# Moving the last batch's first tile forward by one tile, and computing its small second expert on 32 places amid the main one (attention, then a gated mixture of experts, one core)

## The chip, the cores and the metric

The kernel runs on one core of a Trainium2 chip. The metric is device time in microseconds of one execution, lower is better; the median of three runs of the kernel before is 509.26 us (508.65 to 509.94).

## What is computed

Multi-query attention with 8 batches, 16 heads, 384 rows and head size 64 gives 3072 rows of 1024 numbers. Each row then goes to one of 16 experts (4 groups of 4), chosen by two argmaxes; an expert is a two-layer network with a ReLU. Cut to what matters:

```python
attn = softmax(q @ k.T / 8) @ v                 # 8 batches, 16 heads, 384 x 64; one k and v per batch
x = attn.transpose(0, 2, 1, 3).reshape(3072, 1024)
g_idx = argmax(x @ w_group)                     # 4 groups
e_idx = argmax(x @ w_expert[g_idx])             # 4 experts in the group
h = relu(x @ w1[g, e])                          # 1024 x 1024
out = (g_softmax * e_softmax)[:, None] * (h @ w2[g, e])   # 1024 x 1024
```

The inputs are one fixed draw. With it the reference sends all 384 rows of each of batches 0 to 6 to one expert (a different one for most batches), and of batch 7's rows 363 to expert 0 and 21 to expert 2.

## The kernel before

**Tiles and steps.** A tile is 128 rows of one batch, for all 16 heads; there are 24 tiles, t = 0 to 23, three to a batch and in the order of the batches. Each takes four steps of the main loop (L794), so there are 96 steps, i = 0 to 95, with t = i // 4 and p = i % 4. In a step two units are worked on, each two heads of the tile: `scores` (L198, TensorE, L206) puts the scores into one of two PSUM tiles of tag s; `soft` takes the negated row maximum (VectorE, L217) and the exponentials with their sums (ScalarE, L220); `norm` multiplies by the reciprocal sums (GpSimd, L235); and `transp` (VectorE, L241) transposes the units of two steps before into a ring, from which `pv` (TensorE, L257) multiplies them with v, in steps with p of 2 and 3, for the tile before. `pv_out` copies the result out (ScalarE L271, GpSimd L272 into `xb`, the bf16 input of the expert).

**Experts.** In steps with p of 0 and 1 TensorE also works on an expert: `main_expert` is a generator, and `advance(n)` takes 3n portions of it. A batch's expert has 42 portions: three for each of eight 128-wide chunks of the hidden layer (8 matmuls with L479, then a ReLU copy by ScalarE or VectorE, L485/L487), three for each of six pieces of the output (8 matmuls with L493, then a scaled copy into y, L511/L513, and after two pieces the stores, L536). Batch b's expert starts at step 12b + 17, that is 5 steps after the batch's last attention step, so that the 42 portions fit in the steps that follow. The PSUM banks of these matmuls come from a pool of four (`xbank`, tag x) that `pv`, the gate and the expert take in turn; the fifth taker waits until the first one's bank has been read. After the main loop the experts take the s banks instead (`bank_end`).

**Which expert, and when the weights are asked for.** Every batch's main expert is chosen from its first tile alone: `logits` at the batch's step 8, `gate_first`, `gate_choose`, `gate_score` and `gate_pick` at step 9 (L338 to L386), and then `load_main` asks GpSimd's DMA queue for w1 and w2 (L454, two DMAs each, converted to bf16 on the way). The steps are counted from s0 = 12b. The rest of the gate follows when the other two tiles are there (`logits` at s0 + 16, `gate_masks`, `gate_values`, `gate_selected`). For batch 7 a second expert is chosen too (`gate_pick_second`), and its weights are asked for after the main loop (`load_second`, L837 and L844).

**The end, L827 to L908.** After the main loop come the rest of batch 6's expert, the last tile's `pv`, batch 7's gate, batch 7's main expert and, last, the second one. The functions whose names begin with `few_` serve the latter: its rows are gathered into at most 128 places. `few_turn` transposes xb back to rows, `few_flags` and `few_places` give each flagged row its place, `few_gather` (L643) picks the rows with a 0/1 matrix, `few_expert` computes both layers for 128 places (L674, L689) and writes the rows to `out` in DRAM with an indirect DMA by GpSimd (L696). They come after everything else in TensorE's order. Then each engine reads the number of experts left over (L910), and a loop over these (L911) runs as often as that says; in the profiled execution none of its instructions ran.

**What sets the order.** The schedule is by hand: the program's order is each engine's order. `at(step, place, fn, ...)` (L721) puts a function at a step and at one of the places (m0, m1, m3, v, m2, w, e, g) that the loop calls with `run`. "w" stands before `norm`, and "e" and "g" stand behind it.

Of the kernel before, what the change touches and what calls it, by code (L numbers as in the profile page):

```python
# [9 lines left out]
FP32 = mybir.dt.float32  # L10
BF16 = mybir.dt.bfloat16
I32 = mybir.dt.int32
P = 128
# [6 lines left out]
def kernel(  # L20
# [24 lines left out]
    NR = 4096  # L45
    assert NR > N
# [9 lines left out]
    w2f = moe_w2.rearrange("g e (fo fi) d -> (g e) fi fo d", fi=P)  # L56

# [27 lines left out]
    units = [(b, j, c ^ (4 * swapped(b * ST + j))) for b in range(B) for j in range(ST) for c in range(8)]  # L85
# [16 lines left out]
    def load_q(t, first=False):  # L102
        b, j = t // ST, t % ST
# [142 lines left out]
    def pv(t, n0, n1):  # L246

        v_sb = st["v", t // ST]
# [14 lines left out]
    def pv_out(t):  # L263
        b, j = t // ST, t % ST
# [199 lines left out]
    def load_second(n):  # L464
        if n == 0:
            st["e2"] = nc.gpsimd.value_load(st.pop("idx2")[0:1, 0:1], min_val=0, max_val=GE - 1)
        st.setdefault("w_second", []).append(load_w(st["e2"], n))
# [4 lines left out]
    def expert(xb, w1, w2, result, psum, on_act=None):  # L472
# [3 lines left out]
        for fc in range(FO):  # L476
            hp = psum()
            for ko in range(KO):
                nc.tensor.matmul(  # L479
                    out=hp[:, 0:S], lhsT=w1[:, ko, ts(fc, P)], rhs=xb[:, ko, :], start=(ko == 0), stop=(ko == KO - 1)  # L480
                )
                if ko % (KO // 2) == KO // 2 - 1:
                    yield
            if on_act(fc):
                nc.scalar.activation(out=h_t[:, fc, :], in_=hp[:, 0:S], func=ACTF.Relu)  # L485
            else:
                nc.vector.tensor_scalar(out=h_t[:, fc, :], in0=hp[:, 0:S], scalar1=0.0, scalar2=None, op0=ALU.max)  # L487
            yield
# [41 lines left out]

    def main_expert(b, on_act):
        w1, w2 = st.pop(("w", b))

        def store(j, y):
            for n in range(QN):
                nc.sync.dma_start(out=out_v[b, j, n], in_=y[32 * n:32 * (n + 1), :])  # L536

        yield from expert(st["xb", b], w1, w2, scaled(lambda: st["gsel", b][0], store), any_bank, on_act)

    def few_ready():  # L540
# [4 lines left out]
        for name, t, widths in (  # L545
            ("16", c16, (("eye", P), ("tri", P), ("sel", ST * P), ("f", 4), ("cum", 4), ("parts", 5 * ST))),
            ("32", c32, (
                ("cols", P), ("tri", P), ("sel", ST * P), ("prod", ST * GE), ("ohs", GE), ("rows", ST), ("rest", ST), ("row", 1), ("pos", 4),
                ("f", ST), ("fits", 1), ("gate", 1), ("low", 1), ("at", 1),
# [412 lines left out]
```

## Time and profile before

| what | value |
|---|---|
| median of 3 runs | 509.26 us (508.65 to 509.94) |
| the profiled execution's own time | 508.39 us |
| its span (first to last instruction) | 507.0 us |
| granted TensorE clock, mean | 0.997 |
| TensorE, matmuls (PE) | 481.5 us busy, 95% |
| VectorE (DVE) | 413.0 us, 81% |
| ScalarE (ACT) | 321.8 us, 63% |
| GpSimd (POOL) | 289.6 us, 57% |
| bytes moved by DMA | 84.04 MB |

A time in the trace is counted from the span's start. "PE" rows are matmuls, "PEld" rows weight loads, which run beside them. A matmul's row lasts until its last result is written, so the next one starts before it ends: the pace is read from the starts. In the timeline a row merges neighbours: start, length, engine, line, operation, tiles, shapes and count, and in brackets the idle time before it with what ended that. In the chain of work that ended last, each row is a start, a length and what was running.

### The profile page before, as it was taken

To read this page: it belongs to the slowest core of one execution; us is meant where nothing else is said; L and a number is where in the kernel's file an instruction comes from. 1 tells how busy PE (TensorE), PEld (TensorE's weight loads), DVE (VectorE), ACT (ScalarE), POOL (GpSimd) and SP (SyncE) were. 2 spreads that over 40 slices of the span, in tenths; PEclk is the share of its full clock that TensorE was granted. 3 is DMA by queue.
4 is the path that set the end of the run, shared out by engine and by line. 5 is a ranking of instruction groups with operands and counts; after the bars stand their busy time and mean duration, and the time that the engine had idled before them with its cause. 6 is when DMAs were issued, how large, how long until landed. Compare 5 with 4: busy or idle time off the path is not lost.

```text
span 507.0 us, 20054 instructions
## 1 busy us (share of the span) xinstructions
PE 481.5 (95%) x8256; PEld 262.1 (52%) x8273; DVE 413.0 (81%) x737; ACT 321.8 (63%) x1002; POOL 289.6 (57%) x524
## 2 busy tenths in 40 slices
PE   7597789999999999999999999999999999999994
PEld 3143356555456455555465455555455455555653
DVE  3889979988899879988899879998799888890630
ACT  4776766677676766676676776676775775753421
POOL 1665955684576664584576654584476654584300
PEclk9999999999999999999999999999999999999998
DMA  7612997399947998389946998389956993089993
GB/s 106 145 26 45 174 239 193 76 160 233 255 86 129 220 237 218 75 157 232 261 84 123 217 243 223 75 143 230 245 116 111 210 241 110 1 155 241 231 243 121
DMA packets 64524, 84.04 MB, mean 166 GB/s; under 512 B 20379, under 2 KB 39963, under 8 KB 64432
## 3 DMA queue, kind: packets, MB, share of 16 engines
q0 software_dynamic: 19152, 37.84, 41.3%
q1 hardware_dynamic: 44320, 44.61, 35.2%
q8 instruction: 66, 1.08, 0.9%
q10 hardware_dynamic: 960, 0.30, 0.3%
q14 instruction: 26, 0.21, 0.1%
HBM read 101.52 MB, written 19.40 MB: 239 GB/s over the span
## 4 chain that ended last, share of the span: by engine, by line
PE 90%; DVE 5%; ACT 3%; issue 1%; POOL 0%; POOLq 0%; ACTq 0%; DVEq 0%
PE x L257 26%; PE s L206 25%; PE x L479 15%; PE x L493 13%; PE sb L493 4%; PE x L280 3%; ACT pr L220 3%; DVE nmx L217 2%; PE sb L479 2%; DVE ring L241 2%; PE x L674 1%; PE x L100 1%; PE x L689 1%; PE x L145 0%; PE x L643 0%
## 5 line engine op out<-in xcount | busy, mean ns | idle before, releaser
L235 POOL TENSOR_SCALAR pr<-pr,rinv 128x384 f32<-128x384 f32 x384 | 218.3, 588 | 146.0 <-DVE rinv L231 133.2
L220 ACT ACTIVATE pr<-s,nmx 128x384 f32<-128x384 f32 x384 | 218.0, 579 | 131.5 <-DVE nmx L217 120.0
L217 DVE TENSOR_REDUCE nmx<-s 128x2 f32<-128x768 f32 x192 | 174.3, 948 | 45.7 <-PE s L206 44.6
L241 DVE STREAM_TRANSPOSE ring<-pr 128x768 f32<-128x768 f32 x192 | 175.4, 952 | 0.1
L206 PE MATMUL s<-kt,qt 64*64 64x384 f32 x1536 | 148.9, 496 | 13.3 <-ACT pr L220 12.3
L257 PE MATMUL x<-ring,v_sb 32*64 32x256 f32 x4608 | 137.7, 378 | 0.2
L257 PEld LDWEIGHTS x<-ring,v_sb 32*64 32x64 f32 x4608 | 101.6, 131 | 43.0 <-issue 23.2
L206 PEld LDWEIGHTS s<-kt,qt 64*64 64x64 f32 x1536 | 48.5, 132 | 82.6 <-ACT pr L220 44.4
L220 ACT ACTIVATION_READ_ACCUMULATOR pr<-s,nmx 128x1 f32 x384 | 77.9, 203 | 0.0
L479 PE MATMUL x<-xb,w 128*128 128x384 bf16 x448 | 76.6, 326 | 0.0
L479 PEld LDWEIGHTS <-w 128*128 128x128 bf16 x512 | 47.7, 98 | 42.2 <-issue 12.6
L493 PE MATMUL x<-w,h_t 128*128 128x512 bf16 x276 | 64.7, 380 | 0.6
L493 PEld LDWEIGHTS <-h_t 128*128 128x128 bf16 x384 | 35.7, 98 | 52.0 <-issue 11.9
L454 POOL DMA_DIRECT2D w<-in_moe_w_dram x36 | 27.9, 784 | 10.8 <-issue 9.0
L271 ACT COPY xt<-x 128x256 f32<-128x256 f32 x96 | 28.9, 385 | 2.8 <-PE x L257 2.7
L485 ACT ACTIVATE h_t<-x 128x384 bf16<-128x384 f32 x56 | 25.4, 502 | 6.4 <-PE x L479 6.4
L272 POOL CAST xb<-xt 128x1024 bf16<-128x1024 f32 x24 | 24.9, 1036 | 3.6 <-ACT xt L271 3.6
L511 ACT ACTIVATE y<-x,gsel 128x512 f32<-128x512 f32 x36 | 24.8, 693 | 3.1 <-PE x L493 3.1
L195 DVE STREAM_TRANSPOSE qt<-q_sb 128x512 f32<-128x512 f32 x38 | 26.1, 687 | 0.0
L493 PE MATMUL sb<-w,h_t 128*128 128x512 bf16 x92 | 21.2, 379 | 0.2
L231 DVE RECIPROCAL rinv<-ssum 128x4 f32<-128x4 f32 x96 | 13.9, 144 | 3.3 <-ACT pr L220 3.3
L511 ACT ACTIVATE y<-sb,gsel 128x512 f32<-128x512 f32 x9 | 6.2, 688 | 16.1 <-PE sb L493 16.1
(132 smaller groups left out, 165.6 us busy)
## 6 DMA issues: line engine op xcount, KB each, us to landing
w<-in_moe_w_dram POOLq DMA_DIRECT2D x36, 1024.0 KB, 19.6
q_sb<-in_q_dram SPq DMA_DIRECT2D x76, 224.0 KB, 6.0
out_dram<-y SPq DMA_DIRECT2D x96, 128.0 KB, 6.3
xb_scratch<-xb SPq DMA_DIRECT2D x8, 768.0 KB, 4.3
v_sb<-in_v_dram SPq DMA_DIRECT2D x32, 96.0 KB, 4.0
kk<-in_k_dram SPq DMA_DIRECT2D x28, 92.0 KB, 4.1
q_sb<-in_q_dram SPq DMA_DIRECT2D x16, 128.0 KB, 3.3
q_sb<-in_q_dram SPq DMA_DIRECT2D x5, 64.0 KB, 3.1
```

What stands on the lines that cost most here:

```text
L195: nc.vector.transpose(out=qt[:].rearrange("p (x d) -> p x d", d=32), in_=q_sb[:, :, 0:32])
L206: nc.tensor.matmul(out=s[m * D:(m + 1) * D, h, 0:S], lhsT=qt[r, ts(2 * cc + m, D)], rhs=kt[r, :], start=True, stop=True, tile_position=(h ...
L217: nc.vector.tensor_reduce(out=nmx[:], in_=s[:, :, 0:S], axis=AX.X, op=ALU.max, negate=True)
L220: nc.scalar.activation(out=pr[:, h, :], in_=s[:, h, 0:S], func=ACTF.Exp, bias=nmx[:, h:h + 1], scale=1.0, accum_out=ssum[:, k, h:h + 1],)
L235: nc.gpsimd.tensor_scalar(out=pr, in0=pr, scalar1=rinv[:, k, h:h + 1], scalar2=1.0, op0=ALU.mult, op1=ALU.mult)
L241: nc.vector.transpose(out=ring[:, (u // 4) % 3, u % 4].rearrange("p h s -> p (h s)"), in_=st.pop(("pr", u))[:].rearrange("p h s -> p (h s)"),)
L257: nc.tensor.matmul(out=o[i][h * D:(h + 1) * D, 0:2 * P].rearrange("d (g c q) -> d g c q", g=2, c=4), lhsT=v_sb[r, n, :], rhs=ring[r, a:z + ...
L271: nc.scalar.copy(out=xt[:, :, ts(i, 32)], in_=o[:, 0:2 * P].rearrange("p (c q) -> p c q", c=KO))
L454: nc.gpsimd.dma_start(out=w[:, o:o + 4, :], in_=(w1f, w2f)[n][ds(e, 1), :, o:o + 4, :].rearrange("o p c f -> (o p) c f"))
L479: nc.tensor.matmul(out=hp[:, 0:S], lhsT=w1[:, ko, ts(fc, P)], rhs=xb[:, ko, :], start=(ko == 0), stop=(ko == KO - 1))
L493: nc.tensor.matmul(out=yp, lhsT=h_t[:, fo, ts(j, P)], rhs=w2[:, fo, ts(nh, 512)], start=(fo == 0), stop=(fo == FO - 1),)
L511: nc.scalar.activation(out=y[:, ts(nh, 512)], in_=yp, func=ACTF.Copy, scale=g)
```

## The change

Four things change together.

1. **The order of the tiles.** The list `tiles` moves batch 7's first tile ahead of batch 6's third: t = 20 is now (7, 0), t = 21 is (6, 2). `first_slot` and `last_slot` (80 and 92 for batch 7, 72 and 84 for batch 6) replace s0 in the schedule. So batch 7's expert is chosen at step 89 and not at 93; its weights are asked for at steps 89 and 90 (before: 93 and 94). `load_k`, `load_v`, `scale_k` and `k_blocks` of batch 7 move with it; batch 6's later gate steps stay at 92 to 95.
2. **Batch 6's expert in two parts.** It still starts at step 89 with 42 portions, but its input's third tile is now written at the end of step 91. The hidden layer is computed for columns 0 to 255 first (16 portions, in steps 89, 92 and 93) and for columns 256 to 383 then (8 portions of one chunk each, in step 93). TensorE's order shows 32 matmuls of 256 columns in step 89, 24 in step 92, and in step 93 eight of 256 and 64 of 128.
3. **The second expert's weights** are asked for at steps 94 and 95. w2 comes in another layout (`w2r`) and goes to the two q buffers.
4. **The second expert on 32 places, amid the main one.** Its 32 rows are the stationary operand in four column tiles of 32, the weights are the moving one (`few_rows`: 32 matmuls of 256 columns a layer). `few_put` makes the transposed 0/1 matrix, `few_spread` copies each result row to its place in the tile with 12 fp32 matmuls, and the gates and the main expert's rows are joined in SBUF (`last_expert`: y = main * gate + y). The indirect DMA is gone. The ReLU copies of batch 7's expert alternate between ScalarE and VectorE; before, all eight were ScalarE's. The last piece of y is stored by two queues, SP's and ACT's. `keep_xb` of batch 7 goes ahead of its expert.

The diff, cut to its core:

```diff
+    FEW = 32
...
+    w2r = moe_w2.rearrange("g e (fi fo) d -> (g e) fi fo d", fi=P)
...
+    tiles = [(b, j) for b in range(B) for j in range(ST)]
+    tiles.insert(-3, tiles.pop(-3))
+    first_slot = [4 * tiles.index((b, 0)) for b in range(B)]
+    last_slot = [4 * tiles.index((b, ST - 1)) for b in range(B)]
+    units = [(*bj, c ^ (4 * swapped(t))) for t, bj in enumerate(tiles) for c in range(8)]
...
+        halves = [qpool.tile([P, KO // 2, Dm], BF16, tag="q", name="wq", bufs=2) for _ in range(2)]
+        for h, half in enumerate(halves):
+            o = h * (KO // 2)
+            nc.gpsimd.dma_start(
+                out=half[:], in_=w2r[ds(st["e2"], 1), :, o:o + KO // 2, :].rearrange("o p c f -> (o p) c f")
+            )
...
+        for lo, hi, steps in parts:
+            for fc in range(FO):
+                hp = psum()[:, 0:hi - lo]
+                for ko in range(KO):
+                    nc.tensor.matmul(
+                        out=hp, lhsT=w1[:, ko, ts(fc, P)], rhs=xb[:, ko, lo:hi], start=(ko == 0), stop=(ko == KO - 1)
+                    )
+                    if ko + 1 in (KO // 2, KO)[:steps[fc] - 1]:
+                        yield
...
+            *([((0, 2 * P, (3, 2, 2, 2, 2, 2, 2, 1)), (2 * P, S, (1,) * FO))] if b == B - 2 else []),
...
+    def last_expert():
+
+        w1, w2 = st.pop(("w", B - 1))
+        ys = st["ys"] = [pool.tile([P, Dm], FP32, tag="y", name="y", bufs=3) for _ in range(ST)]
+        banks = [bank_end] * FO + [lambda: xbank()[:]] * (2 * ST)
+
+        def result(j, nh, yp, by_act):
+            y, g = ys[j][:, ts(nh, 512)], st["gsel", B - 1][0][:, j:j + 1]
+            if j == 0:
+                nc.scalar.activation(out=y, in_=yp, func=ACTF.Copy, scale=g)
+                return
+            nc.vector.scalar_tensor_tensor(out=y, in0=yp, scalar=g, in1=y, op0=ALU.mult, op1=ALU.add)
+            if j == ST - 1:
+                store_rows(B - 1, j, ys[j], ts(nh, 512), (nc.sync, nc.scalar) if nh else (nc.sync,))
+            elif nh:
+                store_rows(B - 1, j, ys[j])
...
+    def few_rows(lhs, w):
+        bank = xbank()
+        for o in range(KO):
+            for c in range(P // FEW):
+                nc.tensor.matmul(
+                    out=bank[ts(c, FEW), 0:256], lhsT=lhs[:, ts(o, FEW)], rhs=w(o)[:, ts(c, 256)],
+                    start=(o == 0), stop=(o == KO - 1), tile_position=(0, c * FEW),
+                )
...
...
+    def few_hidden():
...
+        bank = few_rows(fw["xg"], lambda o: w1[:, o, :])
+        nc.vector.transpose(
+            out=fw["h32"].rearrange("p (o t) -> p o t", t=FEW), in_=bank.rearrange("p (x o) -> p o x", o=FO)
+        )
+        nc.vector.tensor_scalar(out=fw["h16"], in0=fw["h32"], scalar1=0.0, scalar2=None, op0=ALU.max)
+    def few_out():
...
+        bank = few_rows(fw["h16"], lambda o: halves[o // 4][:, o % 4, :])
+        nc.vector.tensor_copy(out=fw["y32"], in_=bank)
...
+    def few_spread(js):
...
+                nc.tensor.matmul(
+                    out=parts[c // 2][:, c % 2, a:a + 256], lhsT=fw["put32"][r, ts(j, P)], rhs=fw["y32"][r, :],
+                    start=True, stop=True, tile_position=(c * FEW, 0),
+                )
...
+        if last:
+            at(s0 + 9, "w", load_main, b, 0)
+            at(s0 + 10, "w", load_main, b, 1)
+            at(s0 + 13, "w", gate_pick_second, b)
+            at(s0 + 14, "g", load_second, 0)
+            at(s0 + 15, "g", load_second, 1)
...
-    pending.append(main_expert(b, lambda k: k < FO or k % 2 == 0))
+    pending.append(last_expert())
...
     gate_count()
-    advance(1)
+    advance(2)
...
-    advance(3)
     few_gather()
     advance(2)
+    few_put()
+    few_hidden()
+    advance(1)
+    few_out()
+    advance(1)
+    few_spread((0, 1))
+    advance(1)
+    few_spread((2,))
+    advance(1)
...
     advance(1000)
-    keep_xb(b)
-    few_expert()
```

More of the change, by code (lines that the diff above doesn't have):

```diff
@@ L263, in pv_out @@
     def pv_out(t):
[L264 removed]
+        b, j = tiles[t]
         if j < 2:
@@ L683, in few_expert @@
-        cols = ((0, 512), (512, 768), (768, Dm))
-        ys = [xbank()[:, 0:z - a] for a, z in cols]
-        y = pool.tile([P, Dm], FP32, tag="y", name="few_y", bufs=3)
-        for part in range(2):
-            for (a, z), yp in zip(cols, ys):
-                for fo in range(4 * part, 4 * part + 4):
-                    nc.tensor.matmul(
-                        out=yp, lhsT=h_t[:, fo, 0:P], rhs=w2[:, fo, a:z], start=(fo == 0), stop=(fo == FO - 1)
-                    )
-                if part and a:
-                    nc.scalar.activation(out=y[:, a:z], in_=yp, func=ACTF.Copy, scale=gate)
-                elif part:
-                    nc.vector.tensor_scalar(out=y[:, a:z], in0=yp, scalar1=gate, scalar2=None, op0=ALU.mult)
```

192 lines of the change are left out of this document (80 added, 112 removed).

## The prediction

> **What bounds the kernel now.** I read the page first: which engine is busy, and who holds the chain of work that ended last. Then I read the chain's end, and step by step the two stretches that the diff touches.
>
> ```profile
> PE 481.5 (95%) x8256; PEld 262.1 (52%) x8273; DVE 413.0 (81%) x737; ACT 321.8 (63%) x1002; POOL 289.6 (57%) x524
> PE 90%; DVE 5%; ACT 3%; issue 1%; POOL 0%; POOLq 0%; ACTq 0%; DVEq 0%
> ```
>
> TensorE holds nine tenths of the chain, so time taken from its queue is gained and time added is lost, unless another engine is waited for. What matters is the pace of its rows and the few places where it waits. The chain's end (start, length, what):
>
> ```profile
> 481.28 1.34 PE x L643 x24
> 486.20 6.91 PE sb L493 x32
> 493.11 3.57 PE x L674 x64
> 496.95 2.35 PE x L689 x14
> 499.81 0.86 ACT L693 ACTIVATE few_y<-x,c 128x256 f32<-128x256 f32 x2 [2.70 <-PE x L689]
> 501.08 1.05 POOL out_dram L696
> out_dram<-few_y,c POOLq DMA_INDIRECT x1, 2.8
> ```
>
> The second expert stands alone at the end: from 493.11 TensorE does nothing else, ScalarE takes the last piece off by 500.67 (499.81 + 0.86), GpSimd starts the indirect write at 501.02, and it lands 2.8 us later, at 503.8. The span ends at 507.0, 3.2 us behind the landing.
>
> The other stretch is step 93, where batch 6's expert will do nine chunks in place of three. There the profile shows this:
>
> ```profile
> 418.43 1.52 PE L206 MATMUL s<-kt,qt 64*64 64x384 f32 x16
> 423.89 1.52 PE L206 MATMUL s<-kt,qt 64*64 64x384 f32 x16
> 437.19 1.52 PE L206 MATMUL s<-kt,qt 64*64 64x384 f32 x16
> 438.64 2.77 PE L479 MATMUL x<-xb,w 128*128 128x384 bf16 x16
> 439.88 0.21 DVE L290 STREAM_TRANSPOSE lg<-x 128x32 f32<-128x32 f32 x1
> 440.87 0.59 ACT L220 ACTIVATE pr<-s,nmx 128x384 f32<-128x384 f32 x1
> 441.43 0.88 ACT L485 ACTIVATE h_t<-x 128x384 bf16<-128x384 f32 x2
> 442.67 1.52 PE L206 MATMUL s<-kt,qt 64*64 64x384 f32 x16
> ```
>
> TensorE starts the chunks at 438.64, but ScalarE takes the first off only at 441.43, behind the step's four exponentials. The three chunks, 1.3 us each up to 442.67, fit into the four banks, so this delay costs nothing today. The first two rows are the scores of steps 89 and 90; step 89 runs like this one, 18.76 us earlier (418.43 against 437.19).
>
> **The tail, part by part, in the clock of before.** Until the sixth chunk of batch 7's expert nothing changes on TensorE; it is done at about 478.7 (481.28 less two chunks of 1.3). These rows price what follows:
>
> ```profile
> 482.45 0.22 PE L654 MATMUL x<-c 128*128 128x5 bf16 x3
> 468.12 1.10 PE L280 MATMUL x<-xt,wge 128*32 128x64 f32 x64
> 444.12 2.85 PE L257 MATMUL x<-ring,v_sb 32*64 32x256 f32 x96
> L680 DVE TENSOR_SCALAR few_h<-x 128x256 bf16<-128x256 f32 x1 | 0.4, 424 | 1.9 <-PE x L674 1.9
> L513 DVE TENSOR_SCALAR y<-sb,gsel 128x512 f32<-128x512 f32 x3 | 2.3, 751 | 6.9 <-DMA out_dram<-y 2.7 <-PE x L894 2.5 <-PE sb L493 1.7
> 477.27 0.21 DVE L416 TENSOR_REDUCE es<-g_ex 128x15 f32<-128x60 f32 x1
> 482.00 0.35 DVE L887 TENSOR_SCALAR sel<-end,pcum,pw 128x128 bf16<-128x128 f32 x1
> 469.29 0.25 DVE L290 STREAM_TRANSPOSE lg<-x 128x64 f32<-128x64 f32 x1 [12.87 <-PE x L280]
> 493.15 0.75 DVE L513 TENSOR_SCALAR y<-sb,gsel 128x512 f32<-128x512 f32 x1 [2.70 <-DMA out_dram<-y]
> ```
>
> - Gather: 24 matmuls of 32 columns. Of 128 columns they pace at 56 ns (1.34 / 24); three of 5 columns in L654 take 0.22, that is under 40 ns each beyond the last one's run-out. I take 1.0 us (0.9 to 1.34): 479.7. Two chunks of 1.3: 482.3. `few_put`, three at 56 ns: 482.5.
> - `few_hidden`: 32 matmuls in four column tiles of 32. The nearest row is L280, also 32 matmuls in four such tiles, 1.03 us from start to the next start (the row has two records for each). So 1.0 (0.9 for streaming alone, four at once, at the chunks' 384 columns in 0.163 us; 3.5 if they run one after another): 483.5. `few_out` is the same.
> - VectorE now has chunks 1, 3, 5 and 7, a ReLU of 384 columns each: 0.58, between the 0.42 of 256 and the 0.75 of 512. Chunk 5's (478.8 to 479.4) stands ahead of the gate chain, which lasts 5.1 us (477.27 to 482.35, L416 to L887) and includes waits for GpSimd. So it ends at 484.5, and chunk 7's ReLU, queued behind it, at 485.1.
> - Output piece 0 (8 matmuls, 1.73: 6.91 / 4) would run 483.5 to 485.2, but its eighth waits for chunk 7: 485.4. `few_out` waits for `few_hidden`'s transpose (0.42 by L290's 0.25 for 64 columns and 0.69 for L195's 512) and ReLU (0.3) behind that on VectorE: 485.9. So two stalls, 0.7 us together. `few_out` ends at 486.9, piece 1 at 488.6.
> - `few_spread`: 12 fp32 matmuls of 256 columns in four row tiles. L257 does 48 in eight tiles in 2.78, a round of eight in 0.46; a round of four takes the same, so 0.93 and then 0.46. Its copies and joins (two on VectorE, four on ScalarE, about 0.75 each as L513) lie beside pieces 2 and 3. Piece 2 ends at 491.3, the second spread at 491.8, piece 3 at 493.5, pieces 4 and 5 at 497.0.
> - The last join: 0.75, 497.8. SP then issues two stores at 0.42, and ACT two beside it: the last at 498.3. It lands 2.5 us later (2.0 is the least of the 96).
>
> ```profile
> L195 DVE STREAM_TRANSPOSE qt<-q_sb 128x512 f32<-128x512 f32 x38 | 26.1, 687 | 0.0
> L536 SPq DMA_DIRECT2D out_dram<-y x96: 314/419/1085, 113.2 to 495.5; - x96
> DMA to landing us min/median/max: 2.0/6.3/13.9
> out_dram<-y SPq DMA_DIRECT2D x3, 128.0 KB, 2.5
> ```
>
> The landing comes at 500.3 to 500.8, against 503.8; what follows it (3.2) stays. **The tail gains 3.3 us** (2.5 to 4.0). By TensorE alone: it is rid of 7.1 (493.11 to about 500.2, a ScalarE copy before 500.67) and 1.4 of gather, and gets 1.0 + 0.2 + 2.0 + 1.4 and 0.7 of stalls, which is 3.2 less; from its last matmul to the landing it stays at about 3.6.
>
> **Step 93.** Eight chunks of 256 columns pace at 0.87, eight of 128 at 0.45 (8 x 56 ns). Together 10.6 us against 10.4, so the split itself costs 0.2. The banks cost more. Step 93 takes four banks with its first 256-wide and three 128-wide chunks (438.64 + 0.87 + 3 x 0.45 = 440.86; the fourth bank is the logits', free at 440.2 by VectorE's L290, so no wait). The fifth chunk needs the first's bank. ScalarE reads it at 441.43, behind the exponentials, for 0.38 (L682's 256 columns below); so TensorE stands until 441.9. Five chunks of 0.45 then end at 444.15, where the scores of step 94 started at 442.67 before. **Step 93 loses 1.5 us**: 1.0 of waiting and 0.5 of chunks. Step 89 has the 0.4 us less of work, but loses it again: its fourth chunk is the fifth taker (`gate_choose` has a bank too) and waits for ScalarE until 423.05, so it ends at 423.9 as before. Range of this term: 0.5 (no wait) to 2.2.
>
> The Trainium skill's page "TensorE: Matmul & The Clock Gate" (Back-to-back issue gap) gives about 81 ns for a sustained matmul of 128 columns with its weight load. By it the 64 of step 93 would take 5.2 us instead of 3.6, and the sum below would be -0.2 instead of -1.8. L674 in the chain above is 64 matmuls of this very shape, with their loads, in 3.57 us; it gives 56 ns, and I go by it.
>
> ```profile
> L682 ACT ACTIVATE few_h<-x 128x256 bf16<-128x256 f32 x1 | 0.4, 384 | 1.1 <-PE x L674 1.1
> 444.41 1.58 POOL L454 DMA_DIRECT2D w<-in_moe_w_dram  x2 [5.13 <-issue]
> 449.83 4.53 POOL L235 TENSOR_SCALAR pr<-pr,rinv 128x384 f32<-128x384 f32 x8
> 451.45 3.91 DVE L241 STREAM_TRANSPOSE ring<-pr 128x768 f32<-128x768 f32 x4
> 456.41 2.85 PE L257 MATMUL x<-ring,v_sb 32*64 32x256 f32 x96
> DMA to landing us min/median/max: 8.2/19.6/26.7
> L437 POOL TENSOR_TENSOR gate<-gate,gs 128x48 f32<-128x48 f32 x1 | 0.3, 287 | 0.1
> GB/s 106 145 26 45 174 239 193 76 160 233 255 86 129 220 237 218 75 157 232 261 84 123 217 243 223 75 143 230 245 116 111 210 241 110 1 155 241 231 243 121
> ```
>
> **What is moved and costs nothing.** GpSimd waits for the choice and issues the loads ahead of its `norm` (5.13 us idle, 1.58 of issuing); this moves from steps 93 and 94 to 89 and 90. `norm` of 89 then ends some 3 us later, but its transposes come two steps (8 us) later, so it stays hidden. The second expert's loads are behind `gate_values` at step 94 (four small operations like L437, and 1.6 of issuing) and delay `norm` of step 95 to about 456.4, the last transpose to 457.4; the last `pv`, at 456.41 before, is now asked for at 457.9. Hidden by half a microsecond; without that cover it costs up to 1. On VectorE step 93 gets `gate_masks` and `gate_pick_second`, twelve operations of about 0.2 us like L416, and is through at about 444.6, half a microsecond before the next maximum is due (the scores start at 444.15); `gate_selected` at step 95 waits for GpSimd's product (done by then), with only a reciprocal and the transposes behind it. Batch 7's k and v come about a tile earlier too: eight loads on SP, a scaling on GpSimd and one transpose on VectorE (0.6 by L195 and L290), in steps 70 to 76, whose tiles have been read by then; VectorE isn't the bound there. On SP `keep_xb` waits for GpSimd's cast ahead of batch 6's last stores, whose pieces are computed after that cast. The weights: the second expert's w1 is asked for by 454 and w2 by 460, and they are needed at 484.0 and 487.4 (482.5 and 485.9, plus the 1.5 of step 93); the slowest landing of L454 is 26.7. Batch 7's own load moves into a stretch that is free now (the 35th slice, 431 to 444, moves 1 GB/s).
>
> **Sum.** 1.5 - 3.3 = -1.8 us. On the profiled execution: 508.39 - 1.8 = 506.6, a span of 505.2. That execution is 0.87 us below the median of the runs shown, so by the median 509.26 - 1.8: **507.5 us**.
>
> **Rivals.** (a) *The split costs only its columns*: TensorE doesn't stand at step 93, because ScalarE is ahead of where I put it. Then -2.8 to -3.1 (the columns' 0.5 or 0.2): 506.3. For it: TensorE hardly waits for ScalarE today. Against: the fifth taker has no other bank, and the exponentials stand ahead in ScalarE's order. (b) *VectorE becomes the end's bound*: chunk 7's ReLU, `few_hidden`'s two operations and four joins follow the gate chain in one queue, and each microsecond that this is late stops TensorE for as long; with `norm` of 95 late as well, 1.3 us of the gain go: -0.5, 508.8, no change. For it: its 81% of the span, and 0.7 us of stalls by my own count. (c) *The column tiles don't run side by side*: the 64 matmuls of `few_hidden` and `few_out` at 0.108 us are 6.9 us instead of 2.0, which gives +3.1, 512.4, slower. At 0.06 us for a matmul the gain is gone (0.031 + 1.8 / 64), and from 0.083 on it is slower by 0.3%. Against it L280: 64 records in 1.03. The Trainium skill's page "TensorE: Matmul & The Clock Gate" (Part 3, on row and column tiling) says that a weight load overlaps with matmuls in flight only where the row groups differ; here all four tiles share one, which speaks for (c). The trace doesn't bear it out: L280's tiles share the row group too, and its records follow each other at 16 ns (1.03 / 64). (d) *It isn't done as it says*: if over 32 rows were flagged, the expert would go to the loop at the end, with 112 more matmuls (21 us) behind a load (19.6 us): +40. The reference's draw has 21 rows. (e) *The second weights land late*: they would have to take longer than the slowest today; 4 us beyond it give -1.8 + 3.3 (26.7 leaves 0.7 for w2), 510.8.
>
> **How the numbers follow.** Chances: the forecast 0.50, (a) 0.15, (b) 0.22, (c) 0.08, (d) 0.01, (e) 0.04. The forecast's own range is 506.4 to 508.5 (the two terms' ends, rarely both). A measurement of this kernel can tell about 0.3%, 1.5 us, from no change. Two thirds of the forecast and (a) are faster by more: 0.34 + 0.15 = 0.49. The rest of it and (b) are within: 0.38. (c), (d), (e): 0.13 slower. The range leaves out these and the far ends: 505.8 to 510.0.
>
> **What would show it.** Right: in step 93 a gap of about 1 us on TensorE in the middle of the 128-column chunks, ended by ScalarE's ReLU; the column-tiled matmuls of each layer in about 1 us; the last output piece some 3 us earlier against the expert's start than the old `few_expert`'s end; the last store landing about 2.5 us behind its issue. Wrong: no gap at 93 (then a); TensorE waiting for VectorE's transposes or joins by more than 1 us in all (b); pieces of 0.1 us (c); a matmul of the second layer released by a DMA (e).

## The result

The changed kernel takes **512.26 us** (median of 19 runs, 509.67 to 516.03), the kernel before 509.26 (19 runs, 507.51 to 510.62). The ratio is 1.006, with a 95% interval of 1.0042 to 1.0079: it is slower by about 3 us, where 1.8 us less was forecast. Its profiled execution took 513.75 us (span 512.3, granted clock 0.996), against 508.39 (span 507.0, clock 0.997).

The page of the changed kernel, its engines and one group (busy time, mean ns, idle time before it and what ended most of it):

```profile
PE 479.7 (94%) x8320; PEld 262.9 (51%) x8337; DVE 415.9 (81%) x741; ACT 320.8 (63%) x1005; POOL 286.3 (56%) x511
L261 PE MATMUL x<-ring,v_sb 32*64 32x256 f32 x4608 | 137.9, 378 | 3.0 <-issue 2.6
```

TensorE is busy no longer than before (481.5) and yet ends later, so time went into standing still. The rows of what it waited for that bear on this, first of the kernel before, then of the changed one (waiter, releaser: us in total, times, longest). The longest row of both, the scores' waits for ScalarE, is left out; it is 12.3 before and 12.2 now:

```profile
PE s L206 <- issue: 0.8, 1, 0.8
PE x L183 <- issue: 0.7, 1, 0.7
```

```profile
PE x L261 <- issue: 2.6, 3, 1.6
PE x L492 <- ACT h_t L498: 1.2, 2, 0.8
PE x L261 <- DVE ring L245: 0.4, 1, 0.4
```

The wait for ScalarE's ReLU is the forecast one. The waits called "issue" are not: nothing that the profile shows as a semaphore ends them, and all three stand in runs of `pv` matmuls; they follow below. (Two older ones, like the two rows of the kernel before, end at 66 to 75 us in all profiles but those of e7 and d4.) First step 93 of the changed kernel:

```profile
438.85 1.52 PE L210 MATMUL s<-kt,qt 64*64 64x384 f32 x16
440.31 2.39 PE L492 MATMUL x<-xb,w 128*128 128x256 bf16 x32
443.53 2.39 PE L492 MATMUL x<-xb,w 128*128 128x128 bf16 x40 [0.84 <-ACT h_t L498]
445.86 1.52 PE L210 MATMUL s<-kt,qt 64*64 64x384 f32 x16
```

The step lasts 7.00 us (438.85 to 445.86) where it lasted 5.48: 1.52 more, 0.84 of it standing in the middle of the 128-column chunks. Then the tail:

```profile
483.76 0.76 PE L663 MATMUL x<-c,xtok 128*128 128x32 bf16 x24
487.22 1.06 PE L684 MATMUL x<-w,xg 128*32 128x256 bf16 x32
490.72 1.06 PE L684 MATMUL x<-wq,xg 128*32 128x256 bf16 x32 [0.29 <-DVE xg L698]
493.54 1.15 PE L716 MATMUL part<-rest,c 32*128 32x256 f32 x16
494.62 1.90 PE L506 MATMUL x<-w,h_t 128*128 128x512 bf16 x7
495.58 1.35 ACT L726 ACTIVATE y<-part,gsel 128x512 f32<-128x512 f32 x2 [1.24 <-DVE y L728]
496.45 1.22 PE L716 MATMUL part<-rest,c 32*128 32x256 f32 x8
497.61 1.90 PE L506 MATMUL x<-w,h_t 128*128 128x512 bf16 x8
503.13 0.75 DVE L570 SCALAR_TENSOR_TENSOR y<-x,gsel,y 128x512 f32<-128x512 f32 x1 [0.91 <-PEq L945]
503.91 2.25 ACTq L546 DMA_DIRECT2D out_dram<-y  x2
```

A part's price is read from its start to the next part's: gather 0.61, each layer of the small expert 0.99 (487.22 to 488.21, 490.72 to 491.71), first spread 1.08, second 1.16. The last join ends at 503.88. ScalarE's two stores follow at once, SP's two do not:

```profile
507.45 0.78 SPq L546 DMA_DIRECT2D out_dram<-y  x2
```

```profile
SPq L546 <- DMA out_dram<-y: 3.1, 1, 3.1
```

SP stood 3.1 us, until ScalarE's first store had landed (507.38), and its own two landed at 509.06 and 509.52. In the trace the kernel's stores signal their landing on eight semaphores in turn, and SP's next store had the one (number 100) of ScalarE's first: that is what it waited for. The span ends at 512.3, 2.8 us behind the last landing.

So the 5.3 us of span come from these stretches. Up to step 68 the changed kernel is 0.3 ahead (its scores start at 317.64, not 317.92). From there to step 95 (450.13 against 446.90) it loses 3.5: 1.52 in step 93, 1.07 in step 79, 0.66 in step 87, 0.2 in 88, 89 and 92 together. From step 95 to batch 7's second turn of logits (473.23 against 468.12) it loses 1.9, with the 1.57 and the ring's 0.36. From there to the end it takes 39.0 us, not 38.8: of the tail's forecast gain of 3.3 us nothing arrives.

### The profile page after: what moved, and what is told of

Same layout as the page of the kernel before. It is cut to its first block, busy times and chain, and to the rows that moved or that the text cites. A ratio compares the mean times of both kernels' runs of the same rounds, so it can differ in the third digit from the quotient of the medians.

```text
span 512.3 us, 20178 instructions
## 1 busy us (share of the span) xinstructions
PE 479.7 (94%) x8320; PEld 262.9 (51%) x8337; DVE 415.9 (81%) x741; ACT 320.8 (63%) x1005; POOL 286.3 (56%) x511
## 5 line engine op out<-in xcount | busy, mean ns | idle before, releaser
L210 PE MATMUL s<-kt,qt 64*64 64x384 f32 x1536 | 148.9, 496 | 13.5 <-ACT pr L224 12.2
L492 PE MATMUL x<-xb,w 128*128 128x384 bf16 (+2 forms) x512 | 77.1, 306 | 1.2 <-ACT h_t L498 1.2
L506 PE MATMUL x<-w,h_t 128*128 128x512 bf16 x322 | 75.8, 380 | 0.9
L492 PEld LDWEIGHTS <-w 128*128 128x128 bf16 x576 | 51.3, 98 | 40.6 <-issue 14.1
L458 POOL DMA_DIRECT2D w<-in_moe_w_dram x34 | 26.3, 784 | 8.4 <-DVE qt L199 6.0
L498 ACT ACTIVATE h_t<-x 128x384 bf16<-128x384 f32 (+2 forms) x64 | 26.3, 463 | 7.0 <-PE x L492 7.0
L336 POOL TENSOR_TENSOR mask_all<-oh 128x48 bf16<-128x48 f32 x8 | 2.2, 271 | 25.0 <-DVE oh L332 25.0
L284 PEld LDWEIGHTS x<-xt,wge 128*32 128x32 f32 x1024 | 12.8, 110 | 5.5 <-ACT y L524 2.5
```

Source lines behind the costliest of these rows:

```text
L210: nc.tensor.matmul(out=s[m * D:(m + 1) * D, h, 0:S], lhsT=qt[r, ts(2 * cc + m, D)], rhs=kt[r, :], start=True, stop=True, tile_position=(h ...
L458: nc.gpsimd.dma_start(out=w[:, o:o + 4, :], in_=(w1f, w2f)[n][ds(e, 1), :, o:o + 4, :].rearrange("o p c f -> (o p) c f"))
L492: nc.tensor.matmul(out=hp, lhsT=w1[:, ko, ts(fc, P)], rhs=xb[:, ko, lo:hi], start=(ko == 0), stop=(ko == KO - 1))
L498: nc.scalar.activation(out=h_t[:, fc, lo:hi], in_=hp, func=ACTF.Relu)
L506: nc.tensor.matmul(out=yp, lhsT=h_t[:, fo, ts(j, P)], rhs=w2[:, fo, ts(nh, 512)], start=(fo == 0), stop=(fo == FO - 1),)
```

## The experiments

Each ran beside the kernel before on one chip; "before" in the table is its median there.

| run | what it is | median us (runs) | before | ratio, 95% interval |
|---|---|---|---|---|
| e4_order_alone | new order, split and earlier weights; old tail | 511.80 (7) | 509.6 | 1.0030 to 1.0069 |
| e5_tail_alone | new tail, natural order | 521.7 (6) | 509.6 | 1.0205 to 1.0267 |
| e1_sp_alone | changed; last stores on SP alone | 513.46 (6) | 509.6 | 1.0061 to 1.0117 |
| e3_relu_dve | changed; two ReLUs of step 93 on VectorE | 514.2 (6) | 509.6 | 1.0076 to 1.0121 |
| e6_k_early | before; batch 7's k 4 steps earlier | 509.96 (12) | 509.0 | 0.9999 to 1.0037 |
| e7_shifted | changed; +128 TensorE instructions at the start | 526.42 (5) | 509.0 | 1.0303 to 1.0354 |
| e10_whole_block | changed; +256 there | 511.42 (12) | 508.9 | 1.0032 to 1.0081 |
| e8_one_store | changed; a half stored by one DMA | 515.37 (6) | 509.0 | 1.0112 to 1.0160 |
| e9_k_late | changed; batch 7's k back at step 74 | 513.33 (6) | 509.0 | 1.0062 to 1.0137 |
| a0_again | the changed kernel again | 511.56 (12) | 508.9 | 1.0035 to 1.0085 |
| c2_mended | e9 and e1 together | 510.26 (12) | 508.9 | 0.9994 to 1.0041 |
| c1_mended_relu | c2 and e3 | 512.71 (7) | 508.9 | 1.0045 to 1.0097 |
| d1_quarter | c2, +64 instructions behind step 93 | 510.69 (12) | 508.7 | 1.0014 to 1.0054 |
| d2_half | c2, +128 there | 512.57 (6) | 508.7 | 1.0064 to 1.0099 |
| d3_weights_late | c2, second weights later | 510.77 (6) | 508.7 | 1.0029 to 1.0065 |
| d4_relu_half | c1, +128 there | 512.21 (6) | 508.7 | 1.0057 to 1.0098 |

My theories after reading the result: the split's wait in step 93 (B in the expectations); stores at the end that wait for each other (S; SP and ScalarE sharing what the stores signal on); and gaps of TensorE that no semaphore ends (a rival in the first runs, then F if moved transfers make instruction fetches late, G if the place of the instructions does, T if the second weights' transfers do).

**Halving the change.** e4 keeps `before`'s tail and takes the new order; e5 keeps the new tail and drops `tiles.insert(-3, tiles.pop(-3))`, the split and the earlier weights.

> The kernel before (509.26) with the new order of the tiles, batch 6's expert in two parts and batch 7's weights asked for at steps 89 and 90, but with the old end (128 places, indirect write, second weights asked for after the main loop). Theory B (the split alone costs 1.5 us, the earlier request buys nothing, since no matmul waited for these weights): 510.8, step 93 at 7.0 us and the end as before. Rival D (the moved transfers make TensorE's instruction supply stall as well): 512 to 513, with gaps of a microsecond and more that no semaphore ends. Rival G (the earlier weights help the end): below 509.3.

> The changed kernel (512.26) with the natural order of the tiles, batch 6's expert in one part and batch 7's weights at steps 93 and 94 as before; the second expert's weights are asked for right behind them, after the main loop, and the end is the changed one, its two-queue store too. If these weights land in time: step 93 is 5.5 us again and the new end with its late stores is worth 0 to -0.5 against before, 509. If they are late (8 MB asked for within 16 us, at some 230 GB/s until about 490): TensorE waits 2 to 5 us ahead of the second expert's layers, 511 to 514.

e4 is 2.5 us slower than before (511.80 x 0.0049 / 1.0049), nearly all that the whole change loses, and its step 93 has the same 0.84 us of waiting. So the new tail is worth next to nothing on top of it: from the second logits to the end e4 takes 38.8 us, the changed kernel 39.0. The time lies between theory B's 510.8 and rival D's 512 to 513, and D's gaps are there too, at steps 79 and 87 (below). e5 shows what the new order is for:

```profile
PE x L682 <- DMA wq<-in_moe_w_dram: 6.6, 2, 4.2
PE x L682 <- DMA w<-in_moe_w_dram: 2.5, 1, 2.5
```

Without it TensorE stands 9.1 us for the second expert's weights, well over the 2 to 5 us that I expected, and the time is 521.7 where I had 514 at most; in the changed kernel no such wait is left.

**The stores.**

> The changed kernel (512.26) with the last piece of y stored by SP's queue alone, no store from ACT. Theory S (SP's last two stores wait for ACT's stores to land, because they share a completion semaphore out of a rotation of eight): SP's last store is issued 1.4 us after the last join and not 3.9, and lands 2.2 us earlier; time 510.0. Rival W (the writes themselves are slow at the end, whoever issues them): the last landing stays 5.6 us behind the last join, time 512.3. Rival I (stores split over two queues are faster, as written): slower than 512.3.

> The changed kernel with each half of the last piece stored by one DMA of 256 KB on SP, not four of 64 KB, so that the last store waits for no older transfer. Theory S (the stores at the end cost 2.6 us over the prediction, because two of them waited 3.1 us to be issued): the last issue ends 0.5 us after the last join and lands about 3 us after the join, not 5.64, and the time falls by about 2.6 us to 509.7. Rival: one transfer of 256 KB takes as much longer as the wait was, and the last landing stays at 4.3 to 5.6 us after the join, time 511 to 512.3.

```diff
-store_rows(B - 1, j, ys[j], ts(nh, 512), (nc.sync, nc.scalar) if nh else (nc.sync,))
+store_rows(B - 1, j, ys[j], ts(nh, 512))                                # e1
+nc.sync.dma_start(out=out_v[B - 1, j][:, :, ts(nh, 512)], in_=ys[j][:, ts(nh, 512)])  # e8
```

In e1 SP issues all eight half stores without the 3.1 us of standing (the row's end is the last issue):

```profile
500.28 4.37 SPq L546 DMA_DIRECT2D out_dram<-y  x8
500.89 0.75 DVE L570 SCALAR_TENSOR_TENSOR y<-x,gsel,y 128x512 f32<-128x512 f32 x1 [0.91 <-PEq L945]
```

The last one lands at 505.94, 4.3 us behind the last join (501.64) instead of 5.64: the mechanism S is there, but 1.3 us can be had back and not the 2.2 expected, since SP now issues four stores one after another, the last by 504.65, 3.0 us behind the join. And the median of e1 isn't lower than the changed kernel's; what moved its runs by more isn't shown. In e8 both issues end 0.57 us behind the join, but the rival holds, and more than it says: the two transfers keep a quarter of the DMA engines busy for 8 us, and the last packet ends at 510.2, 7.8 us behind the join.

```profile
502.50:510.50 8.00, 0.00 (x0) 0.00 (x0) 0.00 (x0) 0.00 (x0) 0.00 (x0) 0.60 0.24 68
```

The last columns are the DMA share, 0.24, and 68 GB/s: a quarter fits the four entries of this store's outermost dimension, as if each went to one of 16 engines.

**Step 93 by VectorE.**

> The changed kernel (512.26) with the ReLU of step 93's first two chunks on VectorE instead of ScalarE, and the second transpose of batch 6's logits ahead of them. Theory B (the fifth chunk waits for a PSUM bank that ScalarE frees behind four exponentials): the gap of 0.8 us within the 128-column chunks goes, step 93 lasts 6.1 us and not 7.0, time 511.4. Rival P (the 128-column matmuls with their weight loads are slow in themselves): step 93 stays at 7.0, time 512.3. If VectorE is full in step 93, the gap moves to the scores of step 94: 512.3 too.

```diff
-pending.append(main_expert((i - 5) // SB - 1, lambda k: True))
+taken = iter([True] * 7 + [False] * 2 + [True] * 100)   # batch 6; the others as before
+pending.append(main_expert((i - 5) // SB - 1, lambda k: next(taken)))
-at(x + 1, "m0" if b and j0 == 0 else "v", logits_out, b, j0, j1)
+at(x + 1, "m0" if b and (j0 == 0 or b == B - 2) else "v", logits_out, b, j0, j1)
```

```profile
440.01 1.52 PE L210 MATMUL s<-kt,qt 64*64 64x384 f32 x16
441.47 4.62 PE L492 MATMUL x<-xb,w 128*128 128x256 bf16 x72
446.02 1.20 PE L210 MATMUL s<-kt,qt 64*64 64x384 f32 x12
```

The gap is gone and the step lasts 6.01 us, 1.0 less, as theory B says; the 0.5 that is left is the split's columns. But the time isn't lower, here or in c1 below. Both profiles have TensorE waiting for the ring's transposes (0.41 and 0.68 us) and the gap near 466 us, but so has the changed kernel's first profile without the edit; that the edit brings them isn't shown (more on it at the end of this section).

**The gaps that no semaphore ends.** In the changed kernel's profile the three are of 0.44, 0.59 and 1.57 us; here is the longest, and the DMA queues while TensorE stands (packets, MB, share):

```profile
464.69 0.65 PE L261 MATMUL x<-ring,v_sb 32*64 32x256 f32 x7
466.92 2.82 PE L261 MATMUL x<-ring,v_sb 32*64 32x256 f32 x89 [1.57 <-issue]
```

```profile
q0 software_dynamic: 56, 0.11, 60.6%
q1 hardware_dynamic: 57, 0.16, 44.4%
q8 instruction: 1, 0.02, 5.8%
```

One packet of 16,384 bytes on the queue "instruction" starts at 464.46 and takes 0.92 us; TensorE goes on at 466.92. I counted TensorE's instructions in the order of the program (a weight load and a matmul are one each, an fp32 matmul two of each, semaphore instructions count too) and laid the trace beside it. In 18 profiles, all kernels here, there are 70 such gaps over 0.12 us behind 62 us, and every one ends at instruction 256n + 196 to 198. Each ends 2.2 to 2.9 us after the start of such a packet. At the other boundaries behind 75 us, some 1000 in the 18 profiles, the packet started 1.8 us or more ahead, in all but about a dozen 2.2 us or more. So these are the boundaries of instruction blocks, 16,384 bytes for 256 instructions, and TensorE stands when a block's fetch starts less than some 2.2 to 2.9 us ahead of its need. The Trainium skill's page "Runtime: NRT & Kernel Launch" (section Instruction fetch mechanics) says that instructions are refilled in blocks of 16 KiB, 256 instructions, ahead of their use, and that the cost of a boundary is mostly hidden. The trace agrees on the block, and on the cost at the 1000; hidden it isn't, in the 70 cases.

> The changed kernel with 64 small matmuls more (16 behind each of the first four steps, where TensorE waits for ScalarE 0.9 to 1.6 us a step), which shift every later block of TensorE's instructions by half a block, and are worth under 1 us of time themselves. Theory G: the gaps at steps 79 and 87 and the one of 1.57 us near 466 us go, or come up at other steps, and the time moves by 1 us or more, down if fewer late fetches are left. Theory F: the fetches come late at the same steps, since the transfers are the same; the gaps at 79 and 87 stay within 0.4 us of 1.07 and 0.66, and the time is the changed kernel's, 512.3 to 513.

> As the run with 64 small matmuls (16 behind each of the first four steps), but with 128 of them (32 behind each), which are 256 instructions of TensorE: a whole 16 KB block where the other run moved the rest of the program by half a block. Theory G (what a block's boundary falls on decides the gaps): all later blocks lie on the program as in the changed kernel, so the pairs of gaps of 0.6 to 1.5 us in every batch go again and the time falls from 526 back to within 2 us of the changed kernel's, 511.5 to 514.5. Rival (the extra matmuls themselves, or the banks that they take, cost the 14 us): the time is no lower than 526, nearer to 540.

```diff
         run(i, "g")
+        if i < 4:
+            x = xbank()
+            for _ in range(16):   # e10: 32
+                nc.tensor.matmul(out=x[:, 0:32], lhsT=blank[:, 0:P], rhs=blank[:, 0:32], start=True, stop=True)
```

What TensorE waited for, e7 and then e10:

```profile
PE x L261 <- issue: 6.4, 8, 1.3
PE x L284 <- issue: 5.0, 5, 1.5
PE s L210 <- issue: 1.8, 2, 1.1
```

```profile
PE x L261 <- issue: 0.9, 2, 0.6
PE s L210 <- issue: 0.8, 1, 0.8
```

Half a block costs 15 us, with gaps of 0.4 to 1.5 us in pairs in every batch (steps 27 and 28, 39 and 40, and so on). A whole block costs nothing: 511.42, with the unshifted kernel at 511.56 beside it (a0_again below). Neither the matmuls nor the banks matter, only where the boundaries fall. A batch is 2047 instructions (9532 to 11579 from step 60 to 72), eight blocks less one, so what a boundary meets in one batch it meets in all, and the kernel before happens to lie well. That is theory G. But up to step 86 the changed kernel has the same instruction numbers as the one before (12669 at the start of step 79 in both), and step 79 still has its gap, here first in the kernel before and then in the changed one:

```profile
370.90 1.52 PE L206 MATMUL s<-kt,qt 64*64 64x384 f32 x16
372.35 2.85 PE L257 MATMUL x<-ring,v_sb 32*64 32x256 f32 x96
375.13 1.52 PE L206 MATMUL s<-kt,qt 64*64 64x384 f32 x16
```

```profile
370.62 1.52 PE L210 MATMUL s<-kt,qt 64*64 64x384 f32 x16
372.07 1.07 PE L261 MATMUL x<-ring,v_sb 32*64 32x256 f32 x19
373.58 2.41 PE L261 MATMUL x<-ring,v_sb 32*64 32x256 f32 x77 [0.44 <-issue]
375.92 1.52 PE L210 MATMUL s<-kt,qt 64*64 64x384 f32 x16
```

There F is left:

> The kernel before, with batch 7's loads of k, their scaling and their transposes four steps earlier (70, 75, 76), and nothing else: TensorE's instructions and their order are those of before. Theory F (the changed kernel's gaps on TensorE at steps 79 and 87, 1.07 and 0.66 us over before, are late fetches of TensorE's instructions, and the fetches are late because the changed order moves transfers on SP): the steps 79 and 87 get about 0.7 to 1.5 us each longer here too, each after a fetch that starts late, and the time is about 511. Rival G (the gaps come from TensorE's own new order of instructions, which puts the blocks of a fetch at other places): both steps stay within 0.1 us of before, and the time is before's, 509.5.

> The changed kernel with batch 7's loads of k back at step 74 (scaling 77, transposes 78), so that TensorE's instructions and their order are unchanged and SP's transfers around step 76 stand as before. Theory F: the gap at step 79 goes (1.0 us or more less than in the changed kernel), that at 87 is open, and the time is about 511. Rival G: both gaps stay, time 512.3. If k comes too late, step 80 shows a wait for kt instead.

```diff
-at(s0 - 10, "g", load_k, b)
+at(s0 - (6 if last else 10), "g", load_k, b)        # e9; scale_k 5 -> 3, k_blocks 4 -> 2
```

Lengths of steps against the kernel before (scores to scores; a stall can be longer than the idle row says, as the ends of matmuls are modelled), and the gap near 466 us:

| profile | k at step | step 79 | step 87 | gap near 466 |
|---|---|---|---|---|
| after, a0_again | 70 | +1.07, 0 | +0.66, +0.77 | 1.57, 0 |
| e1, e3 | 70 | +0.71, +0.65 | +0.81, +0.93 | 0, 1.40 |
| e4, e8, e10 | 70 | +1.53, +0.79, +0.92 | +0.90, +0.90, +0.67 | 0, 0, 0 |
| e9, d3 | 74 | 0, 0 | +0.50, +0.50 | 1.56, 0 |
| c1, c2, d1 | 74 | 0, 0, 0 | 0, 0, 0 | 1.40, 0, 0 |
| d2, d4 (other boundary) | 74 | 0, 0 | 0, 0 | 0.74, 0.99 |
| e6 (natural order) | 70 | +0.24 | 0 | 0.73 |
| e5 (natural order) | 74 | 0 | 0 | 0.33 |

With k at 70 step 79 is longer in six of seven profiles of the new order, with k at 74 in none of seven; step 87 goes from seven of seven to two of seven, and by less. In the changed kernel the fetch for step 79 starts at 370.79, 0.17 us into the step, in the kernel before at 369.17, 1.73 us ahead of it. In instructions, that fetch starts 48 to 71 ahead of its boundary in the six profiles, and 138 to 170 ahead in the seven with k at 74. So k's earlier place does make this fetch late (F), by the loads or by what moves with them (the scaling and the transposes). e6 misses F's forecast: 0.24 at step 79, nothing at 87, and a time not told from before's; so k's place is needed but not enough. What on the queues delays a fetch isn't shown. Busy DMA engines go with late fetches. No fetch starts more than 297 instructions ahead of its boundary; counted from there, over the 18 profiles, it starts 0.5 us later (median) where the DMA engines were under a tenth busy in that microsecond, and 4.2 us later where they were over nine tenths busy. But at step 79 they are full in the kernel before as well. e9 as a whole is a miss: its median isn't lower (513.33); its profile has the gap near 466.

> The changed kernel once more, beside the mended ones on the same chip, for a second profile: 512.3 as before; the gaps at steps 79 (about 1.0) and 87 (0.66 to 0.9) come again if they belong to the program, and the one of 1.57 us near 466 may be there or not.

> The changed kernel with batch 7's k back at step 74 and the last piece stored by SP alone. Both theories together (late fetches from moved transfers; stores that wait): step 79 is 1.0 us shorter, the last landing comes 4.3 us behind the last join and not 5.6, and the time is 512.3 - 1.0 - 1.3 = 510.0. Rival (the single runs of both edits were no faster than the changed kernel, so what they save comes back as gaps elsewhere): 512.3 or more.

> The same with step 93's first two ReLUs on VectorE and batch 6's second turn of logits four places later, so that TensorE doesn't wait for ScalarE there. Theory B (the split costs step 93 a wait of 0.84 us for the bank and 0.5 us of added instructions): step 93 is 1.0 us shorter than in the run beside it and the time 1.0 less, 509.0, about the kernel before. Rival: no faster than the run beside it, since VectorE's edit delays something else.

a0_again says that the gaps at 79 and near 466 come in some executions of one and the same kernel: this profile has neither, and its execution took 510.03 us, 3.7 less than the one shown above (from step 95 to the second logits 20.6 us, not 23.1). c2 came out as forecast, 510.26: 1.3 us below the changed kernel beside it, and not to be told from the kernel before. But each of its two edits alone (e1, e9) was no faster than the changed kernel, so its profile, and not the sum of theirs, says what the pair does. Its step 79:

```profile
372.42 1.52 PE L210 MATMUL s<-kt,qt 64*64 64x384 f32 x16
373.87 2.85 PE L261 MATMUL x<-ring,v_sb 32*64 32x256 f32 x96
376.65 1.52 PE L210 MATMUL s<-kt,qt 64*64 64x384 f32 x16
```

4.23 us, no gap, as before. c2 also says what is left of the miss when neither the late fetches nor the wait between two queues is there: from step 68 to the end its profile takes 189.4 us, the kernel before 189.0, and 187.2 was forecast. Step 93 costs its 1.5 as forecast; the tail gains 1.1 (37.7 us from the second logits on, 38.8 before) and not 3.3, with the last landing still 4.5 us behind the last join. c1 is a miss: step 93 is 1.0 us shorter than in c2 and the median 2.5 longer; in its profile the stretch from step 95 to the second logits, with the gap near 466, is 2.6 us longer than in c2's (23.24 against 20.61).

> The mended kernel (batch 7's k at step 74, last piece stored by SP alone) with 32 small matmuls behind step 93: every later block boundary lies 64 instructions earlier in the program. Theory G: the boundary that had the gap of 1.5 us (instruction 16068) now falls on other work, the gap there goes or comes at another boundary, and the runs lie closer together or further apart, with a median up to 1.5 us from the 510.3 of the mended kernel; the matmuls themselves cost at most 0.9 us (26 ns each). Theory T (the gap comes from the transfers of the second weights): no change beyond 0.9 us.

> The same with 64 small matmuls, 128 instructions, half a block, at most 1.7 us of their own. Theory G: another pattern of gaps behind step 93 than in the mended kernel and in the run with 32, medians 508.5 to 513. Theory T: 510.3 to 512.

> The mended kernel with the first half of the second weights asked for one step later and the second half behind the last transposes, about 8 us later. Theory T: fetches of instructions between 450 and 470 start sooner, the gap near 466 never comes, median 509.5 or less, unless TensorE then waits for the second weights (bound: they landed 5.7 us before few_out began, so up to 3 us). Theory G: the gap comes or not as before, 510.3, plus the wait.

> The mended kernel with the ReLU edit (VectorE, step 93) and with 64 small matmuls behind step 93. If the ReLU edit's 1.0 us was only hidden by the gap near 466 and the wait for the ring, and the shift takes the gap away: 1.0 us less than the run with 64 alone. If the edit itself brings the executions with the gap: no faster than that run.

```diff
+        if i == NSL - 3:                        # d1: 32 matmuls of 32 columns, d2 and d4: 64
+            ...
-at(s0 + 14, "g", load_second, 0)               # d3: at s0 + 15; load_second(1) ahead of few_ready()
```

The small matmuls cost 0.8 and 1.6 us in step 93, as bounded, and the boundaries behind it move: d1 has no gap over 0.1 us from there on, d2 one of 0.74 at another boundary (16324), d4 two (0.78, 0.99). So no shift pays: d1 isn't told from c2, and d2 and d4 are slower. d4 isn't told from d2. In d3 the gap near 466 doesn't come, as T says, but neither does it in c2, and the median, 510.77, isn't under T's 509.5.

The traces do say what goes with the gap near 466. The eleven profiles of the new order without d1, d2 and d4 part by the fetch of the block before. Where that had started 3.1 us or more before TensorE came within 264 instructions of the boundary (seven profiles), the next fetch starts right there, and there is no gap. Where it had started 3.0 us or less before (four: after 3.0, e9 3.0, e3 2.3, c1 1.9), the next starts only some 16 instructions ahead of the boundary, 11.7 to 12.6 us behind the one before, and TensorE stands. In all four the DMA engines were idle (share 0.01 or less) from 1 us ahead of that place to 1.5 us behind it, which speaks against T. e3 and c1 lie lowest: the microsecond saved in step 93 brings TensorE to the place sooner, and the fetch before it comes no sooner, which would explain why that edit doesn't pay. The dividing line is drawn after the fact, and why the fetch before is later in some executions stays open.

## Why the prediction was wrong, step by step

- *Step 93, "loses 1.5 us"*: right, 1.52, by 0.84 of waiting for the first bank and the rest in columns (rival (a) is out; e3 takes the wait away and 1.0 us goes). The Trainium skill's page "TensorE: Matmul & The Clock Gate" (Back-to-back issue gap) has about 81 ns for such a matmul with its load; the last five chunks, 40 of them, take 2.33 us (443.53 to 445.86), 58 ns each.
- *"Step 89 ... ends as before"*: nearly; it is 0.19 longer, with a wait of 0.41. The steps 88 and 92 change by -0.34 and +0.36.
- *Gather 1.0*: 0.61, 25 ns for a matmul of 32 columns. *The layers 1.0 each*: 0.99. Rival (c) is out: 31 ns a matmul, though all column tiles share a row group.
- *Two stalls, 0.7 together*: 0.78 by the starts of the matmuls, 0.31 ahead of piece 0's eighth (chunk 7's ReLU) and 0.47 ahead of `few_out`.
- *Spread 0.93 and 0.46*: 1.08 and **1.16**. The second spread writes the same tile of PSUM as the first and waits for ScalarE's copy (495.58), which had itself waited 1.24 us for VectorE's two joins. That 0.7 is most of the 0.8 us by which the expert's start to the end of the last join took longer than forecast (29.48 us from 474.40, against 28.65: 497.8 less 469.15, where the expert starts before).
- *"SP then issues two stores at 0.42, and ACT two beside it: the last at 498.3. It lands 2.5 us later"*: **failed**. A gain of 3.3 means a landing at 500.5, 2.7 us behind the last join; it was 5.64, because SP's two stood 3.1 us for ScalarE's store. (The term was also short by its own rows: two issues of 0.42 one after the other end at 498.6, not 498.3, and with 2.5 to the landing the gain is 2.7.) Taken together, 0.8 + 2.9 less 0.4 (the end comes 2.8 us behind the landing, not 3.2) is 3.3: the whole gain of the tail. With SP alone the landing still comes 4.3 to 4.5 us behind the join (e1, c2), so the wait between the queues is only a part of what this term left out; the other part is four issues on one queue.
- *"`norm` of step 95 ... hidden by half a microsecond"*: gone in some executions (0.36 us for the ring), within the 1 us named.
- *"What is moved and costs nothing ... Batch 7's k and v come about a tile earlier too"*: **failed**. I counted queues and buffers, and not TensorE's own instruction fetches among the transfers. That costs 0.8 to 2.4 us at steps 79 and 87 (in all seven profiles of the new order with k at 70). Another late fetch, near 466, costs about 2 more in some executions; that k's place causes that one isn't shown, since it comes with k at 74 as well.
- *Rivals*: (d) and (e) did not happen, and nothing waits for the second weights. (b) is there in small: VectorE sits behind the ring's 0.36 and the second spread's 0.7. No rival held the two causes that decided. With both mended (c2) the kernel is still 1.3 us above the one before by the medians, within the noise, and not 1.8 below.

Of the 7.1 us between the forecast -1.8 and the 5.3 of the profiled execution, 3.5 are the tail (39.0 less 38.8, and the 3.3), 1.7 are steps 79 and 87, and 1.9 the stretch with the gap near 466; the rest cancels. The median lies 1.5 us below that execution; a0_again's, without the gaps at 79 and 466, lies 3.7 below.

## What to carry to other kernels

A store at the very end is priced by what its issue may have to wait for, not by its issue and landing alone: several queues are no gain if one waits for another's transfers. With all eight stores on one queue the last landed 1.3 us sooner behind the last join here (4.3 us against 5.64), though that edit alone didn't lower the median. In an unrolled kernel that keeps TensorE busy all the time, look for gaps that "issue" ends, and for the instruction fetches ahead of them: any edit that adds instructions or moves transfers can make or remove such gaps far from where it was made, so compare an edit in more than one profile and try a shift of the program before judging it.

## What the runs showed that I had not expected

- TensorE's instructions arrive in blocks of 256, and half a block's shift at the start costs 15 us of 512 (526.42 against 511.42 for a whole block).
- One and the same kernel has gaps in one execution and not in the next: 510.03 and 513.75 us, both at a clock of 0.996.
- A store of 128 rows written as 4 x 32 x 512 keeps a quarter of the DMA engines busy: two halves, 512 KB, took 8 us.
